# Attention, MoE and MoE on one core: half of block 0's loads into other tiles, and banks of their own for the last output sums

## The chip, the cores and the metric

The kernel runs on one core of a Trainium2 chip. A core has five engines that work side by side, each through its own instructions in order: TensorE (PE; its weight loads are listed as PEld), VectorE (DVE), ScalarE (ACT), GpSimd (POOL) and SyncE (SP, which here only issues DMAs). The metric is the device time of one execution in microseconds, the median over the runs shown; lower is better.

## What is computed

The reference chains three layers and returns float32; the MoE weights are float64:

```python
def reference(q, k, v, n_global, n_local, moe, moe2):
    x = attention(q, k, v)               # (2, 8, 768, 64): global keys < 8, local window of 96
    x = x.transpose(0, 2, 1, 3).reshape(1536, 512)
    h = x @ moe.w_in                     # 512 -> 2048
    P = a[0] + a[1] * h + a[2] * h**2 + a[3] * h**3
    Q = 1 + abs(b[0]) * abs(h) + abs(b[1]) * h**2
    x = (P / (Q + 1e-6)) @ moe.w_out     # 2048 -> 512
    h = x @ moe2.w_in                    # 512 -> 1024
    s = h * softmax(h)
    ln = (s - mean(s)) / sqrt(var(s) + 1e-6) * g_ln
    return ln @ moe2.w_out               # 1024 -> 512
```

Scores are masked to the first 8 keys and to the 96 keys up to the query's own, and get a bias that falls with the distance, with a slope of its own for each head.

## The kernel before

The 1536 tokens are cut into 12 tiles of 128. The **attention** of one tile is four units, each a pair of heads, numbered from 0 in the order in which they come: units 0 to 11 are block 0 (tiles 0 to 2), 12 to 23 block 1, and so on, four blocks of 384 tokens. A unit is loaded by two DMAs (`u_load`, lines 438 to 444): `qk`, its queries and keys, and `v`, its values. `u_front` multiplies them on PE (`L459`), takes the scores with bias and their extreme on DVE (`L464`), the exponential on ACT (`L471`), the reciprocal of the sum on DVE (`L476`, `L477`), and scales by it (`L482`) on DVE for the units in `NDVE` (3 to 11 among them) and on POOL for the others. `u_back` transposes (`L502`), copies (`L514`, ACT), multiplies by the values (`L509`), and copies the result into `x` as a high part (`L516`, ACT) and a remainder (`L99`, DVE).

**MoE 1** goes block by block over 16 slices of the hidden width. The high and low parts of the inputs and of the weights are multiplied apart (`L634`, `L636`, `L640`), the quotient P/Q is made on ACT, DVE and POOL (lines 660 to 679), and its product with the second weights (`L725`, `L726`, `L731`) sums in three PSUM banks. Block 0 does half of its slices first, is written to memory, and does the other half last. Weights come as 64-bit words, 512 KB for each DMA (`L541`), into four tiles `wst`, and are turned into float32 by ACT and DVE (`L565` to `L586`) and split into high (`L604`, ACT) and low (`L99`, mostly POOL).

**MoE 2** goes over the 12 tiles, in the order 3 to 11 and then 0 to 2; below they are counted from 0 in that order. For each: transposes of the input (`L791`), the hidden sums in two halves of 12 matmuls (`L810` to `L812`, `p2_h`), softmax and normalisation on DVE and ACT (`L832` to `L854`), eight transposes in two pieces of four (`L872`, `p2_tr`) with copies (`L880`) and remainders (`L99`), and the output sum of 24 matmuls in bank `y2` (`L894` to `L896`, `p2_o`), which ACT copies out (`L903`) for a DMA (`L905`). The last tile's sum is made in two halves of 256 columns.

**What sets the order.** `record` writes down every step as an operation with its engine, a length, the values that it reads and writes, and for new values the pool that they take a buffer from. `Plan.run` then goes through a list of ready operations and takes those whose turn comes first, by due times worked out backwards from the end; that writes each engine's order. Buffers are handed out from pools: `qk` has 3, `v` 4, `t` 9, `y` 4, `wst` 4; PSUM banks are pools too: `h` and `s` two each, `p`, `y0`, `y1`, `y2` one each. Values of one `line` get their buffers in the order in which they were written down. Where the plan leaves PE idle in its first 30 us, `fill` (`L337`) puts in small matmuls on the identity into a free bank; one of them in the source is two instructions of the trace. A load of a later weight is held until the hidden sum of the step before has run (`after`, line 541).

Four of the `t` tiles, t0 to t3, hold the tables from which the attention's bias is made (lines 383 to 417); apart from that `t` serves MoE 1's quotient, and `y` its finished sums.

## Time and profile before

| | us |
|---|---|
| median of 3 runs | 559.95 |
| lowest and highest | 559.59, 560.86 |
| the profiled execution | 558.11 |
| its span, first to last instruction | 556.3 |
| PE busy | 531.8 (96%), 2910 instructions |
| DVE busy | 446.0 (80%) |
| ACT busy | 393.0 (71%) |
| POOL busy | 182.5 (33%) |
| DMA, mean over the span | 101 GB/s |

A busy time is the time in which an engine has an instruction under way. The granted clock of PE is full for the whole of the work. The span has attention of block 0 up to about 44 us, MoE 1 with the attention of the other blocks beside it up to about 290, MoE 1 alone with the weights of MoE 2 up to about 400, and MoE 2 to the end. Times in the rows below are microseconds from the start of the span.

### The profile page before, as it was taken

How to read it: one execution, taken by the hardware profiler on the slowest of the kernel's cores; microseconds unless marked ns; L12 is line 12 of the kernel's file. 1: busy time of each engine (PE TensorE's matmuls, PEld its weight loads, DVE VectorE, ACT ScalarE, POOL GpSimd, SP SyncE). 2: the span in 40 equal slices, each digit the busy share in tenths (PEclk: the TensorE clock that was granted, in tenths of full speed). 3: DMA queues.
4: the chain of work that ended last, by engine and by line, in shares of the span. 5: the costliest groups of instructions: out<-in, count | busy, mean ns of one | idle time of the engine just before them, and what ended most of it. 6: DMA issues, size and time to landing. Idle time of an engine off the chain costs nothing.

```text
span 556.3 us, 8937 instructions
## 1 busy us (share of the span) xinstructions
PE 531.8 (96%) x2910; PEld 437.0 (79%) x2910; DVE 446.0 (80%) x1104; ACT 393.0 (71%) x911; POOL 182.5 (33%) x212
## 2 busy tenths in 40 slices
PE   7999999999999899999999999999999999999995
PEld 6668776877788678778788887888878788888874
DVE  4997999999999999878788999999876755455530
ACT  5688999898888878787778988898544543334330
POOL 2311665546456632122342644674510000000000
PEclk9999999999999999999999999999999999999999
DMA  7469662544354432211013322252101111000011
GB/s 252 130 201 341 195 219 86 185 135 153 104 182 154 151 96 98 73 48 48 1 38 114 133 77 75 77 180 87 57 20 38 39 38 58 20 19 20 19 39 43
DMA packets 28278, 56.24 MB, mean 101 GB/s; under 512 B 3520, under 2 KB 11968, under 8 KB 28224
## 3 DMA queue, kind: packets, MB, share of 16 engines
q1 hardware_dynamic: 28080, 55.59, 30.9%
q8 instruction: 25, 0.41, 0.3%
q14 instruction: 29, 0.24, 0.1%
q10 hardware_dynamic: 144, 0.00, 0.0%
HBM read 47.72 MB, written 7.86 MB: 100 GB/s over the span
## 4 chain that ended last, share of the span: by engine, by line
PE 55%; DVE 29%; ACT 10%; issue 4%; DMA 1%; POOL 0%; SPq 0%; ACTq 0%; DVEq 0%; POOLq 0%
PE pb L894 4%; PE pb L896 4%; PE pb L895 4%; PE pb L634 4%; PE pb L810 4%; PE pb L812 4%; PE pb L811 4%; PE pb L640 4%; PE pb L731 3%; PE pb L636 3%; PE pb L725 3%; DVE t L667 3%; PE pb L459 3%; DVE wst L574 3%; PE pb L726 3%
## 5 line engine op out<-in xcount | busy, mean ns | idle before, releaser
L99 POOL TENSOR_TENSOR g<-t,g 128x384 fp32r<-128x384 f32 x64 | 69.2, 1082 | 103.9 <-ACT g L677 91.7
L634 PE MATMUL pb<-x,w 128*128 128x384 f32 x256 | 89.3, 349 | 1.8 <-DVE t L667 1.8
L636 PE MATMUL pb<-x,w 128*128 128x384 f32 x256 | 86.1, 336 | 0.0
L725 PE MATMUL pb<-w,g 128*128 128x512 f32 x192 | 77.5, 404 | 4.2 <-ACT g L677 4.2
L726 PE MATMUL pb<-w,g 128*128 128x512 f32 x192 | 75.6, 394 | 0.5 <-POOL w L99 0.5
L99 POOL TENSOR_TENSOR w<-wst,w 128x512 fp32r<-128x512 f32 x42 | 57.2, 1364 | 42.7 <-ACT w L604 38.8
L640 PE MATMUL pb<-x,w 128*128 128x384 f32 x256 | 58.0, 347 | 0.1
L731 PE MATMUL pb<-w,g 128*128 128x512 f32 x192 | 57.7, 409 | 0.2 <-POOL g L99 0.2
L634 PEld LDWEIGHTS pb<-x,w 128*128 128x128 f32 x256 | 48.1, 188 | 8.6 <-DVE t L667 4.4
L471 ACT ACTIVATE e<-e,st 128x256 f32<-128x256 f32 (+1 forms) x96 | 46.3, 486 | 6.4 <-DVE st L464 6.4
L640 PEld LDWEIGHTS pb<-x,w 128*128 128x128 f32 x256 | 44.5, 188 | 7.1 <-issue 3.1
L636 PEld LDWEIGHTS pb<-x,w 128*128 128x128 f32 x256 | 48.1, 188 | 1.5
L725 PEld LDWEIGHTS pb<-w,g 128*128 128x128 f32 x192 | 36.0, 187 | 14.4 <-ACT g L677 7.3
L660 ACT ACTIVATE t<-pb,coef 128x384 f32<-128x384 f32 x64 | 42.7, 668 | 6.1 <-PE pb L640 6.1
L482 POOL TENSOR_SCALAR e<-e,st 128x256 f32<-128x256 f32 (+1 forms) x58 | 28.0, 495 | 54.4 <-DVE st L477 48.4
L669 ACT ACTIVATE t<-t,coef 128x384 f32<-128x384 f32 x64 | 39.6, 618 | 6.8 <-DVE t L667 6.6
L662 DVE TENSOR_TENSOR t<-t,pb 128x384 f32<-128x384 f32 x64 | 35.2, 549 | 11.1 <-ACT t L663 6.5
L677 ACT CAST g<-t 128x384 fp32r<-128x384 f32 x64 | 32.8, 512 | 16.0 <-DVE t L675 15.3
L880 ACT CAST lh<-pb 128x512 fp32r<-128x512 f32 x24 | 13.9, 592 | 42.5 <-PE pb L872 42.5
L459 PE MATMUL pb<-qk 64*128 64x256 f32 (+3 forms) x192 | 41.3, 393 | 2.7 <-DVE st L464 1.0
L667 DVE SCALAR_TENSOR_TENSOR t<-pb,coef,t 128x384 f32<-128x384 f32 x64 | 39.2, 613 | 5.2 <-ACT pb L666 4.8
L671 DVE SCALAR_TENSOR_TENSOR t<-t,t 128x384 f32<-128x384 f32 x64 | 40.6, 634 | 1.3 <-ACT t L670 1.3
(113 smaller groups left out, 1293.2 us busy)
## 6 DMA issues: line engine op xcount, KB each, us to landing
wst<-in_w_in SPq DMA_DIRECT2D x24, 512.0 KB, 4.0
wst<-in_w_out SPq DMA_DIRECT2D x24, 512.0 KB, 3.7
qk<-in_qkv SPq DMA_DIRECT2D x40, 256.0 KB, 2.7
v<-in_qkv SPq DMA_DIRECT2D x40, 128.0 KB, 2.5
y_d<-y SPq DMA_DIRECT2D x12, 256.0 KB, 2.5
y<-y_d SPq DMA_DIRECT2D x12, 256.0 KB, 2.6
out<-wst SPq DMA_DIRECT2D x11, 256.0 KB, 2.0
qk<-in_qkv SPq DMA_DIRECT2D x8, 192.0 KB, 3.7
```

The source lines that it names most:

```text
L99: eng.tensor_tensor(out=out, in0=a, in1=hi.bitcast(F32), op=ALU.subtract)
L459: pe.matmul(out=score(h), lhsT=a[r, h * 128:(h + 1) * 128], rhs=a[r, 256:256 + w], start=True, stop=True)
L471: act.activation(out=e[:, h, 0:w], in_=e[:, h, 0:w], func=AF.Exp, scale=-1.0, bias=st[:, h:h + 1], accum_out=st[:, 2 + 2 * h:3 + 2 * h])
L634: pe.matmul(out=pb[:, g.h.slot, 0:n], lhsT=wt[wh.slot][:, cs[p]], rhs=xt[x[p][0].slot][:, 0:n], start=(p == 0), stop=False)
L636: pe.matmul(out=pb[:, g.h.slot, 0:n], lhsT=wt[wl.slot][:, cs[p]], rhs=xt[x[p][0].slot][:, 0:n], start=False, stop=False)
L640: pe.matmul(out=pb[:, g.h.slot, 0:n], lhsT=wt[wh.slot][:, cs[p]], rhs=xt[x[p][1].slot][:, 0:n], start=False, stop=(p == 3))
L660: op("ACT", 0.2 + 0.46 * k, lambda: act.activation(out=T(g.c), in_=h(), func=AF.Identity, scale=coef[:, 3:4], bias=coef[:, 2:3]), r=[g.h], ...
L667: op("DVE", 0.2 + 0.41 * k, lambda: stt_(out=T(g.a), in0=h(), scalar=coef[:, 5:6], in1=T(g.b), op0=ALU.mult, op1=ALU.add), r=[g.h, g.b], n ...
L671: op("DVE", 0.15 + 0.41 * k, lambda: stt_(out=T(g.a), in0=T(g.a), scalar=1.0 + 1e-6, in1=T(g.b), op0=ALU.add, op1=ALU.mult), r=[g.b], w=[g ...
L725: pe.matmul(out=pb[:, y[i].slot, :], lhsT=gt[g.gh.slot][:, c], rhs=wt[wh.slot], start=g.first, stop=False)
L726: pe.matmul(out=pb[:, y[i].slot, :], lhsT=gt[g.gh.slot][:, c], rhs=wt[wl.slot], start=False, stop=False)
L731: pe.matmul(out=pb[:, y[i].slot, :], lhsT=gt[g.gl.slot][:, c], rhs=wt[wh.slot], start=False, stop=g.last)
```

## The change

In block 0 every second unit (odd numbers) loads its `qk` into a tile of pool `y` and its `v` into one of pool `t`. The values have lines of their own there (`qk0`, `v0`). In `p2_h` the first half of a tile's hidden sum takes both of its banks and the second half writes on, and the sums wait until all weights but the last two have been scaled (`scaled[:-2]`). In `p2_o` the tile before the last sums in bank `y1`, and the second half of the last one in a bank of pool `s`. The branch `ROOT`, another way to make Q, is off, so its code is left out here, and an unused tile `cf` of four columns is added.

```diff
+ROOT, EARLY, ENDS = False, (0,), True
...
+    def aside(u):
+        return u.j in EARLY and u.k % 2 == 1
+
+    def qk_of(u):
+        return yt[u.qk.slot] if aside(u) else qkt[u.qk.slot]
+
+    def v_of(u):
+        return tt[u.v.slot] if aside(u) else vt[u.v.slot]
+
     def u_load(u):
-        u.qk, u.v = Val("qk"), Val("v")
+        u.qk, u.v = (Val("y", "qk0"), Val("t", "v0")) if aside(u) else (Val("qk"), Val("v"))
...
-    nconv, nlo = [0], [0]
+    nconv, nlo, scaled = [0], [0], []
...
-        op("ACT", 0.63, scale, r=[st], new=[bank] + list(new), lead=WLEAD, tag="wsc")
+        scaled.append(op("ACT", 0.63, scale, r=[st], new=[bank] + list(new), lead=WLEAD, tag="wsc"))
...
-               new=[o.h[half]] if half else [o.h[0]], occ=2.76, tag="h2")
+               **{"w" if half else "new": o.h[1:] if half else o.h}, occ=2.76, after=scaled[:-2], tag="h2")
...
-        b, ot = Val("y2"), Val("wst", "ot")
+        ot = Val("wst", "ot")
+        bs = [Val("y2")] if n == 1 else [Val("y2"), Val("s" if ENDS else "y2")]
+        if ENDS and o.k == NTILE - 2:
+            bs = [Val("y1")]
+        if n == 2 and not ENDS:
+            bs[1] = bs[0]
```

Since the plan is made anew, the order of all engines moves. Three places follow. On SyncE, after the two small loads at the start of the program, the order before was (`qk0` to `qk2` and `v0` to `v3` are the buffers of a unit's two loads, `wst` a weight):

```order
L441 DMA qk0_204<-in_qkv 128x384
L441 DMA qk1_205<-in_qkv 128x384
L441 DMA qk2_206<-in_qkv 128x384
L443 DMA v0_207<-in_qkv 128x128
L443 DMA v1_208<-in_qkv 128x128
L443 DMA v2_209<-in_qkv 128x128
L443 DMA v3_210<-in_qkv 128x128
L541 DMA wst0_156<-in_w_in 128x1024
L541 DMA wst1_157<-in_w_in 128x1024
L541 DMA wst2_158<-in_w_in 128x1024
L441 DMA qk0_204<-in_qkv 128x384
```

The same place on SyncE now (lines 473 and 475 are 441 and 443):

```order
L473 DMA qk0_204<-in_qkv 128x384
L473 DMA y0_189<-in_qkv 128x384
L473 DMA qk1_205<-in_qkv 128x384
L473 DMA y1_190<-in_qkv 128x384
L473 DMA qk2_206<-in_qkv 128x512
L475 DMA v0_207<-in_qkv 128x128
L473 DMA y2_191<-in_qkv 128x512
L475 DMA t4_164<-in_qkv 128x128
L475 DMA v1_208<-in_qkv 128x128
L475 DMA t5_165<-in_qkv 128x128
L473 DMA y3_192<-in_qkv 128x512
L473 DMA qk0_204<-in_qkv 128x512
```

Unit 3's `qk` has moved from behind three weights to the fourth place, and the first weight comes ten rows later than before.

On VectorE, behind the reciprocal of unit 2, the order before was (`x` a unit's result, `e3` and `st3` the scores and sums of unit 3; 569 to 574 are a weight's conversion):

```order
L99 TENSOR_TENSOR x1_174<-pb_89,x0_173 128x128
L569 SCALAR_TENSOR_TENSOR pb_89<-pb_89,wst0_156 128x512
L570 SCALAR_TENSOR_TENSOR pb_89<-wst0_156,pb_89 128x512
L99 TENSOR_TENSOR x3_176<-pb_89,x2_175 128x128
L574 SCALAR_TENSOR_TENSOR wst0_156<-wst0_156,pb_89 128x512
L99 TENSOR_TENSOR x5_178<-pb_89,x4_177 128x128
L569 SCALAR_TENSOR_TENSOR pb_89<-pb_89,wst1_157 128x512
L570 SCALAR_TENSOR_TENSOR pb_89<-wst1_157,pb_89 128x512
L464 ISA e3_214,st3_219<-pb_89,bt6_202 128x128
```

The same place on VectorE now:

```order
L496 ISA e3_214,st3_219<-pb_89,bt6_202 128x128
L496 ISA st3_219 128x1
L496 ISA e3_214,st3_219<-pb_89,bt7_203 128x128
L496 ISA st3_219 128x1
L103 TENSOR_TENSOR x1_174<-pb_89,x0_173 128x128
L496 ISA e0_211,st4_220<-pb_89,bt0_196 128x256
L496 ISA st4_220 128x1
L496 ISA e0_211,st4_220<-pb_89,bt1_197 128x256
L496 ISA st4_220 128x1
L508 TENSOR_SCALAR st3_219<-st3_219 128x2
```

The conversions of two weights have left this place, and units 3 and 4 have come forward.

On TensorE, between the output sums of tiles 8 and 9 of MoE 2, the order before was (`lh0`, `lh1` and `ll0`, `ll1` are the two tiles' transposed inputs, `wst0` the normalised rows of tile 10):

```order
L894 MATMUL pb_89<-w31_123,lh0_2943 128x512
L895 MATMUL pb_89<-w30_122,lh0_2943 128x512
L896 MATMUL pb_89<-w31_123,ll0_2945 128x512
L872 MATMUL pb_89<-ident_65,wst0_156 128x128 x4
L894 MATMUL pb_89<-w17_109,lh1_2944 128x512
L895 MATMUL pb_89<-w19_111,lh1_2944 128x512
```

The same place on TensorE now:

```order
L942 MATMUL pb_89<-w30_122,lh0_2925 128x512
L943 MATMUL pb_89<-w31_123,ll0_2927 128x512
L941 MATMUL pb_89<-w17_109,lh1_2926 128x512
L942 MATMUL pb_89<-w19_111,lh1_2926 128x512
L943 MATMUL pb_89<-w17_109,ll1_2928 128x512
```

The four transposes between the two sums have moved ahead of both.

## Rows read from the trace of the kernel before

**Rows 1.** By stage: stretch, length; PE, PEld, DVE, ACT, POOL busy; clock; DMA share; GB/s.

```profile
7.86:20.00 12.14, 11.00 (x84) 8.38 (x82) 8.85 (x35) 10.33 (x35) 4.75 (x9) 1.00 0.72 257
20.00:43.66 23.66, 22.76 (x176) 16.04 (x176) 22.09 (x97) 18.08 (x64) 5.05 (x7) 1.00 0.60 185
43.66:60.00 16.34, 15.69 (x106) 13.03 (x104) 12.93 (x39) 14.17 (x39) 4.28 (x6) 1.00 0.84 289
60.00:200.00 140.00, 133.21 (x748) 107.43 (x747) 136.19 (x332) 124.95 (x299) 80.85 (x96) 1.00 0.49 154
200.00:290.00 90.00, 90.00 (x525) 72.28 (x524) 75.48 (x201) 72.37 (x174) 25.39 (x29) 1.00 0.19 58
430.00:544.00 114.00, 112.79 (x554) 93.71 (x552) 61.19 (x147) 46.16 (x94) 0.00 (x0) 1.00 0.09 31
```

**Rows 2.** Timeline of PE in block 0: start, duration, line, operation, count.

```profile
16.00 0.49 PE L459 MATMUL pb<-qk 64*128 64x128 f32 x4
16.42 2.27 PE L337 MATMUL pb<-ident 128*128 128x128 f32 x18
...
43.66 0.42 PE L634 MATMUL pb<-x,w 128*128 128x384 f32 x1
```

**Rows 3.** DMA issues of SyncE; last row: landing times of `L441` up to 20 us.

```profile
4.97 1.38 SPq L541 DMA_DIRECT2D wst<-in_w_in  x3
6.61 0.33 SPq L441 DMA_DIRECT2D qk<-in_qkv  x1
...
DMA to landing us min/median/max: 2.7/3.8/6.0
```

**Rows 4.** Waits of DVE, 7.5 to 44 us: total us, times, longest.

```profile
DVE x L99 <- ACT x L516: 1.2, 3, 0.7
DVE e L464 <- ACT bt L417: 1.2, 3, 0.5
DVE st L476 <- ACT e L471: 1.1, 3, 0.4
DVE pb L569 <- ACT pb L565: 0.8, 1, 0.8
```

**Rows 5.** Timeline of DVE in block 0, rows of normalisations and of one reduction.

```profile
19.17 1.55 DVE L482 TENSOR_SCALAR e<-e,st 128x128 f32<-128x128 f32 x2
...
37.38 1.64 DVE L482 TENSOR_SCALAR e<-e,st 128x256 f32<-128x256 f32 x2
...
42.98 0.41 DVE L464 CUSTOM_DVE_ANT_0 e<-pb,bt 128x256 f32<-128x256 f32 x1
...
43.77 0.17 DVE L476 TENSOR_SCALAR st<-st 128x2 f32<-128x2 f32 x1
...
44.24 0.61 DVE L482 TENSOR_SCALAR e<-e,st 128x256 f32<-128x256 f32 x2
```

**Rows 6.** Timeline of POOL at the same times.

```profile
19.38 1.27 POOL L99 TENSOR_TENSOR w<-wst,w 128x512 fp32r<-128x512 f32 x1 [0.51 <-ACT w L604]
...
37.60 1.27 POOL L99 TENSOR_TENSOR w<-wst,w 128x512 fp32r<-128x512 f32 x1 [12.80 <-ACT w L604]
```

**Rows 7.** Timeline of PE in MoE 2, with idle time before and its releaser.

```profile
408.69 1.09 PE L872 MATMUL pb<-ident,wst 128*128 128x128 f32 x8 [0.77 <-DVE wst L854]
...
432.45 0.66 PE L872 MATMUL pb<-ident,wst 128*128 128x128 f32 x4 [0.80 <-DVE ll L99]
...
531.60 0.50 PE L894 MATMUL pb<-w,lh 128*128 128x512 f32 x1 [0.24 <-ACT wst L903]
...
543.44 0.39 PE L896 MATMUL pb<-w,ll 128*128 128x512 f32 x1
544.50 0.39 PE L894 MATMUL pb<-w,lh 128*128 128x256 f32 x1 [0.68 <-ACT wst L903]
```

**Rows 8.** Timelines of ACT and SyncE in MoE 2.

```profile
424.42 1.12 ACT L859 ACTIVATE pb<-wst,st 128x1024 f32<-128x1024 f32 x1 [2.40 <-DVE st L839]
...
550.91 0.81 SPq L905 DMA_DIRECT2D out<-wst  x2
```

More of the change, by code (lines that the diff above doesn't have):

```diff
@@ L417, in bias_pair, with root_log, root_end @@
             act.mul(bt[h], dz, -8.0 * SLOPE[h])
+    vcf = Val()
+    cf = const.tile([128, 4], F32, name="cf")
+    def root_log():
+        act.activation(out=cf[:, 1:2], in_=cf[:, 0:1], func=AF.Ln)
+        act.activation(out=cf[:, 1:2], in_=cf[:, 1:2], func=AF.Exp, scale=0.5)
+    def root_end():
+        dve.reciprocal(out=cf[:, 2:3], in_=cf[:, 1:2])
+        dve.scalar_tensor_tensor(out=cf[:, 1:2], in0=cf[:, 0:1], scalar=cf[:, 2:3], in1=cf[:, 1:2], op0=ALU.mult, op1=ALU.add)
+        dve.tensor_scalar(out=cf[:, 1:2], in0=cf[:, 1:2], scalar1=0.5, scalar2=None, op0=ALU.mult)
+        dve.reciprocal(out=cf[:, 2:3], in_=cf[:, 1:2])
+        dve.tensor_tensor(out=cf[:, 3:4], in0=cf[:, 2:3], in1=coef[:, 4:5], op=ALU.mult)
     op("POOL", 0.9, bias_iota, new=vt0)
@@ L508, in pv @@
                     v0 = k * 128 + h * 64
-                    pe.matmul(out=pb[h * 64:(h + 1) * 64, u.xp.slot, 0:128], lhsT=vt[u.v.slot][:, v0:v0 + 64],
+                    pe.matmul(out=pb[h * 64:(h + 1) * 64, u.xp.slot, 0:128], lhsT=v_of(u)[:, v0:v0 + 64],
                               rhs=ptt[:, c:c + 128], start=(k == 0), stop=(k == n - 1))
@@ L659, in e_ops @@
         stt_ = dve.scalar_tensor_tensor
-        op("ACT", 0.2 + 0.46 * k, lambda: act.activation(out=T(g.c), in_=h(), func=AF.Identity, scale=coef[:, 3:4], bias=coef[:, 2:3]),
-           r=[g.h], new=[g.c], tag="c")
-        op("DVE", 0.14 + 0.41 * k, lambda: dve.tensor_tensor(out=T(g.c), in0=T(g.c), in1=h(), op=ALU.mult), r=[g.h], w=[g.c], tag="ch")
-        op("ACT", 0.15 + 0.42 * k, lambda: act.activation(out=T(g.b), in_=h(), func=AF.Abs, scale=coef[:, 4:5]), r=[g.h], new=[g.b], tag="abs")
@@ L899, in p2_o @@
         cs = [slice(i * w, (i + 1) * w) for i in range(n)]
-        parts = [op("PE", 5.52 / n + 0.3, lambda c=c: mm(c), r=[o.lh, o.ll] + [v for f in range(8) for v in W["o2", f]],
-                    **{"w" if i else "new": [b]}, occ=5.52 / n, tag="o") for i, c in enumerate(cs)]
         for i, c in enumerate(cs):
-            op("ACT", 0.59 / n, lambda c=c: act.copy(wst[ot.slot].bitcast(F32)[:, c], pb[:, b.slot, c]), r=[b],
+            b = bs[i]
+            op("PE", 5.52 / n + 0.3, lambda c=c, b=b: mm(c, b), r=[o.lh, o.ll] + [v for f in range(8) for v in W["o2", f]],
+               **{"w" if i and b is bs[0] else "new": [b]}, occ=5.52 / n, tag="o")
+        for i, c in enumerate(cs):
+            b = bs[i]
+            op("ACT", 0.59 / n, lambda c=c, b=b: act.copy(wst[ot.slot].bitcast(F32)[:, c], pb[:, b.slot, c]), r=[b],
                **{"w" if i else "new": [ot]}, tag="ot")
```

36 lines of the change are left out of this document (27 added, 9 removed).

## Prediction

> **What bounds the kernel now.** I read the busy time by stages first [rows 1], then the first 44 us on TensorE, SyncE and VectorE, then the waits of TensorE in MoE 2. In [rows 1] the binding engine changes from stage to stage. From 60 to 200 us VectorE is busy for 136.19 of 140 us; from 200 to 290 us TensorE for 90.00 of 90, and from 430 to 544 us for 112.79 of 114. Neither kind of stretch can take in a delay: what reaches 60 us earlier or later reaches the end earlier or later, unless the order of work behind it changes. Slack that a reordering can win lies ahead of that: VectorE is busy for 8.85 of the 12.14 us up to 20 us, and for 12.93 of 16.34 between 43.66 and 60 us.
>
> The first stretch is the attention of block 0, twelve units. TensorE starts the first hidden matmul of MoE 1 at 43.66 us, when the last of them is done [rows 2]. TensorE is not what sets that: it runs fillers, for instance 18 instructions in 2.27 us ahead of the scores of unit 4 [rows 2], 0.126 us each. The loads have a part in it. The score tiles have three buffers, so the load of unit 3 is issued at 6.61 us, after the first score matmul, and behind three weight loads of 512 KB; loads of this line take 2.7 to 6.0 us to land in the first 20 us [rows 3], so it may land as late as 12.6. Its matmul runs at 16.00 us [rows 2]. VectorE fills part of this hole with weight conversions. So the hole is not all lost time, and its price is what VectorE really waited: from 7.5 to 44 us 1.2 us for the copy x of a unit (`L516`), 1.2 for the bias tables, 1.1 for exponentials and 0.8 for a weight's scaling [rows 4], 4.3 in all.
>
> **The change part by part.** *Loads of block 0.* The counts of compute instructions and DMAs stay as they are; only 19 pairs of fillers fall away (32 for 51). Units 1, 3, 5, 7, 9 and 11 load into y and t tiles, so only half of the units still take turns in the three score and four value buffers, and seven units are on their way before the first weight. On SyncE the first weight load now stands behind 17 loads of units in place of 7. Three issues there take 1.38 us [rows 3], so the ten more make it 10 x 0.46 = 4.6 us later. Its conversion has moved on VectorE too, behind the scores of unit 7, and is hidden by them. If it landed later still, VectorE would wait in its order, and units 8 to 11, which come next on it, with it.
>
> On VectorE the score reductions now follow each other. Of the 3.1 us that were not spent on the bias tables (those stay: ScalarE's order is unchanged up to there) I take 1.8 as won. The bounds are 0 (each wait turns up at another reciprocal, since the chain of reduction, exponential and reciprocal is as long as before) and 3.1; I take the middle, somewhat up, since the later waits on `L516` fall when more units are in flight.
>
> Two units of block 1 leave this stretch too. Before, the reductions of units 12 to 15 stand ahead of the last rounding remainder of block 0, now those of 12 and 13 alone. The reductions of one unit take from 42.98 to 43.77 us, 0.79, and its reciprocal two instructions of 0.17 [rows 5]: two units and one reciprocal are 1.9 us, which move behind the start of MoE 1. There VectorE has 16.34 - 12.93 = 3.4 us of idle time [rows 1], which hides them; without that cover they would cost 1.9 again. So the first hidden matmul comes 1.8 + 1.9 = 3.7 us earlier, at about 40.0 us. The fillers say much the same from the other side: 19 pairs at 2 x 0.126 = 4.8 us less of hole to fill.
>
> One cost in this stretch goes by luck. The normalisation of a unit on VectorE takes 0.61 us for two instructions, but 1.55 and 1.64 where GpSimd subtracted a weight's halves at the same time (from 19.38 and from 37.60, 1.27 each); in both cases they end together [rows 5, 6]. That is about 1.0 us twice. Four such subtractions stand in this stretch, before and now. I leave it at two meetings; none would give 2 us more, four take 2 us.
> [...]
>
> *Order in MoE 2.* The first half of the hidden sums now claims both banks, and the order there changes much, on TensorE, which has no slack: each wait is paid in full. Before, 24 hidden matmuls, transposes, and 24 output matmuls alternate. Now halves of 12 are parted by transposes, and three times two output sums follow each other on bank y2, which ScalarE must empty between. The second and third (tiles 1 and 2, tiles 5 and 6) have a transpose between them, as tiles 8 and 9 had before, where the wait was 0.24 us [rows 7]; tiles 8 and 9 now have nothing between, as the last two sums had, 0.68 us [rows 7]. That is 2 x 0.24 + 0.44 = 0.9 us. Transposes of a tile that come three pieces in a row waited 0.80 us once for a bank [rows 7]; now there are two such places, 0.8 us more. The wait of 0.77 us for the first normalised tile [rows 7] goes, since those transposes now stand a half later. Together +0.95 us; bounds -0.8 and +3.5, since a copy can also stand behind a square of 1.12 us on ScalarE [rows 8].
>
> *Banks of the last sums.* Tile 10 sums in y1 and the second half of tile 11 in a bank of its own. The first matmul of tile 11 started at 544.50, 1.06 us after the last of tile 10 in place of the usual 0.23 [rows 7]: 0.83 us go. The copy of its first half is then done while the second is summed, and the last output DMA, now the second of a pair that SyncE issues in 0.81 us [rows 8], goes half of that, 0.4 us, sooner. That is -1.23 us, with little doubt.
>
> **The sum.** -3.7 + 0.95 - 1.23 = -4.0 us on the profiled execution of 558.11 us (span 556.3 and 1.8 around it): 554.1. The median of the runs, 559.95, lies 1.84 us above that execution, so the forecast is 556.0.
>
> **The rivals.** *The early gain is hidden anyway.* The weights wait instead of the units: conversions that VectorE did in the hole, where it was busy for 8.85 us [rows 1], must be done later, in a stretch where it is busy for 22.09 of 23.66 us, and the chain of reduction, exponential and reciprocal, not the load, turns out to have set the pace; of the waits nothing is won, and the two moved reductions push the first activations of MoE 1 back by as much. Then about 0.6 us of the 3.7 is left: 559.95 - 0.6 + 0.95 - 1.23 = 559.1. For it: only 3.1 us of wait are there at all. Against it: 19 pairs of fillers fewer, and the 3.4 us of idle time after 43.66 us.
>
> *MoE 2 gives it back, and more.* This is the slower case. Three places with output sums in a row and three with transposes in a row each wait not 0.24 to 0.80 us but for a copy, a remainder and a 1.12 us square in ScalarE's queue, some 1.1 us more each: 6 x 1.1 = 6.6, so 562.6. It turns slower than before by 0.2% when those six cost 5.1 us more than counted, 0.85 each. For it: TensorE has 1.2 us of idle time in 114 there, so the order before was better than one can expect of a new one. Against it: ScalarE is busy for 46.16 of 114 us, so the queue is mostly short [rows 1].
>
> [...] All four subtractions meet a normalisation: 558.0, still faster; none: 554.0.
>
> *The change does not do what it says:* a load of block 0 into a t tile could wait for the bias tables, which live in t0 to t3 at first. The order excludes it but for unit 11, whose turn comes long after.
>
> **How the numbers follow.** Forecast with its spread of port meetings 0.70, all of it faster; hidden gain 0.16, of which 0.13 within 0.2% and 0.03 faster; MoE 2 gives back 0.14, of which 0.02 ends within 0.2% and 0.12 slower. A measurement of this kernel tells about 0.2% (1.1 us) from no change. So faster 0.73, same 0.15, slower 0.12. The range: all bounds in the good direction (no port meeting, 3.1 us of waits won, MoE 2 at -0.8) give 556.0 - 2.0 - 1.3 - 1.75 = 551.0, all in the bad one over 561. I cut both by what seldom comes together: 552.3 to 560.4.
>
> **What would show it.** Right: the score matmul of unit 3 near 10 to 11 us, the first hidden matmul near 40 us, VectorE above 9.5 of 12.14 us in the first stretch, 60 us reached with the same MoE 1 work done as before at 63 to 64, and no wait of the last sum near its start. Wrong: a first hidden matmul at 43 us (the loads did not matter), VectorE idle for longer than 3.4 us right after it (the moved work was not hidden), normalisations of 1.5 us in more than two places, or TensorE below 111 of 114 us in MoE 2. Waits of TensorE on the copy `L903` beyond 1.2 us in total would show the order there as the price.

## The result, and the profile after

The change made the kernel slower: 566.09 us median of 4 runs (564.62 to 566.16), where the kernel before has 559.85 (559.59 to 560.86), a ratio of 1.0108 (1.0086 to 1.0129). The forecast was 556.0 with a range of 552.3 to 560.4, so direction and range were both wrong. The profiled execution took 566.08 us; its span is 563.9 us, 7.6 more than before. (The medians are 6.2 us apart. The profiled execution of before, 558.11 us, lies 1.7 under its median, that of after on its median.) TensorE is busy for 531.9 us (531.8 before), although it has 38 filler instructions less to run (2872 instructions for 2910): slower work at the start (2.1 us) and near 188 us (an estimated 1.7 us, below) fills most of their place, and the 7.6 us are idle time.

The lines of before have other numbers now: `L99` is `L103`, `L459` `L491`, `L464` `L496`, `L514` `L546`, `L516` `L548`, `L574` `L606`, `L634` `L666`, `L662` `L704`, `L667` `L709`, `L725` `L767`, `L872` `L914`, `L894` `L941`, `L903` `L953`; kernels with edits further up have 3 to 7 more. The stages, with the columns of [rows 1]:

```profile
7.86:20.00 12.14, 11.90 (x80) 8.84 (x80) 6.79 (x41) 9.59 (x39) 2.16 (x6) 1.00 0.97 317
41.67:60.00 18.33, 16.15 (x108) 13.84 (x107) 15.08 (x49) 15.83 (x42) 7.82 (x12) 1.00 0.79 261
60.00:200.00 140.00, 129.60 (x728) 105.19 (x727) 133.21 (x321) 121.22 (x292) 79.39 (x92) 0.99 0.47 146
200.00:290.00 90.00, 89.94 (x522) 71.80 (x521) 76.23 (x202) 71.80 (x173) 25.29 (x28) 1.00 0.20 62
430.00:544.00 114.00, 111.39 (x541) 91.71 (x540) 62.62 (x154) 46.15 (x95) 0.00 (x0) 1.00 0.09 31
```

Against [rows 1], VectorE (the third busy time) has lost 2 us at the very start (6.79 for 8.85) and 3 us between 60 and 200 us, where it is the engine that sets the pace (133.21 for 136.19). TensorE has lost 1.4 us in MoE 2 (111.39 for 112.79).

**The start.** The timeline of TensorE, then a row of VectorE and the first hidden matmul:

```profile
5.65 0.80 PE L491 MATMUL pb<-qk 64*128 64x128 f32 x4 [1.05 <-DMA qk<-in_qkv]
6.38 4.63 PE L341 MATMUL pb<-ident 128*128 128x128 f32 x20
10.94 0.58 PE L491 MATMUL pb<-y 64*128 64x128 f32 x4
...
41.67 0.52 PE L666 MATMUL pb<-x,w 128*128 128x384 f32 x1
```

```profile
11.66 0.29 DVE L496 CUSTOM_DVE_ANT_0 e<-pb,bt 128x128 f32<-128x128 f32 x1 [3.00 <-PE pb L491]
```

The 20 fillers between the scores of units 0 and 1 took 4.63 us, 231 ns each. In the profile of before the same 20 took 2.50 us, from 5.84 on. Unit 1's scores stand behind them in TensorE's order, so VectorE waited 3.00 us for these scores. Even so the first hidden matmul came 2.0 us earlier than in [rows 2].

**MoE 1.** What VectorE waited for from 100 to 200 us, after (total us, times, longest):

```profile
DVE t L709 <- ACT pb L708: 1.5, 3, 0.7
DVE x L103 <- ACT x L548: 1.0, 3, 0.6
DVE t L704 <- ACT t L702: 0.5, 2, 0.3
DVE t L704 <- ACT t L705: 0.4, 1, 0.4
DVE st L508 <- ACT e L503: 0.2, 1, 0.2
```

and the same of before:

```profile
DVE t L667 <- ACT pb L666: 0.8, 3, 0.4
```

That is 3.6 us in place of 0.8. Near 188 us the granted clock of TensorE also fell, to 0.58 over 4 us. Its timeline, and the windows around it (columns as in [rows 1]):

```profile
186.56 0.66 PE L541 MATMUL pb<-pt,v 128*64 128x128 f32 x8 [0.73 <-ACT pt L546]
188.59 0.77 PE L767 MATMUL pb<-w,g 128*128 128x512 f32 x1 [1.37 <-ACT g L719]
189.16 0.63 PE L768 MATMUL pb<-w,g 128*128 128x512 f32 x1
189.59 0.63 PE L767 MATMUL pb<-w,g 128*128 128x512 f32 x1
```

```profile
184.00:188.00 4.00, 2.10 (x16) 1.33 (x16) 3.96 (x8) 3.02 (x7) 1.28 (x1) 1.00 0.68 231
188.00:192.00 4.00, 3.41 (x10) 2.75 (x11) 3.93 (x9) 2.80 (x7) 3.16 (x4) 0.58 0.41 125
```

From 188.6 to 192.0 us the granted clock is 0.51, and the matmuls of `L767` and `L768` start 0.43 us apart and not 0.23 as at 198 us. Ahead of that lies a stretch in which TensorE worked for 2.10 of 4 us, at 1.00. Estimated from the clock, 3.4 us x (1 - 0.51), the same work would take 1.7 us less at 1.00. Of the four runs of the change, the three near 566.1 us have a mean granted clock of 0.993 or 0.994, and the one of 564.62 us has 1.000.

**The end of MoE 1, and MoE 2.** Rows of TensorE's timeline, with its longest waits there and the start of the last two output sums:

```profile
376.83 0.44 PE L666 MATMUL pb<-x,w 128*128 128x384 f32 x1 [1.58 <-DVE t L709]
...
418.93 0.47 PE L852 MATMUL pb<-w,yh 128*128 128x512 f32 x1 [1.12 <-DVE wst L606]
...
439.55 0.66 PE L914 MATMUL pb<-ident,wst 128*128 128x128 f32 x4 [0.79 <-DVE ll L103]
...
459.33 0.50 PE L941 MATMUL pb<-w,lh 128*128 128x512 f32 x1 [0.85 <-ACT wst L953]
...
509.14 0.50 PE L941 MATMUL pb<-w,lh 128*128 128x512 f32 x1 [0.24 <-ACT wst L953]
...
540.72 0.50 PE L941 MATMUL pb<-w,lh 128*128 128x512 f32 x1 [0.73 <-ACT wst L953]
...
552.49 0.39 PE L943 MATMUL pb<-w,ll 128*128 128x512 f32 x1
552.72 0.28 PE L941 MATMUL pb<-w,lh 128*128 128x256 f32 x1
```

The last output sum starts 0.23 us behind the sum before it, where [rows 7] had 1.06: that part of the change does what it should.

Where the same step has the same matmuls in both kernels, its start can be followed through the span. After minus before: first hidden matmul -2.0 us; 40th of MoE 1's 64 hidden steps (280 us) +4.7; last hidden step of MoE 1 +5.4; output sum of tile 10 +9.1; last sum +8.2; last matmul +8.1; end +7.6. So the front gained 2.0, MoE 1 up to 200 us lost 6.7, what lies between 300 us and tile 10 lost 4.4, and the banks at the end won back 1.5.

**Where the front's gain went.** It was gone by the 4th hidden step, which starts at 55.67 us before and at 57.49 after. VectorE from the first hidden step to the 4th, and from the start of the span to the 26th (198.11 us before, 202.80 after), each time before and then after:

```profile
43.66:55.67 12.01, 8.83 (x28) 1.00 0.99 343
0.00:198.11 198.11, 181.81 (x519) 1.00 0.55 176
```

```profile
41.67:57.49 15.82, 12.64 (x41) 1.00 0.83 279
0.00:202.80 202.80, 181.88 (x519) 0.99 0.54 171
```

Between the first and the 4th step VectorE works 3.8 us longer than before and is idle for the same 3.18 us: what had moved behind the first hidden matmul was not taken up by idle time there. Up to the 26th step it has run the same 519 instructions with the same busy time, so the 4.69 us by which this step comes late are its idle time, 20.92 us for 16.30. Of the 4.62 us more, 1.69 lie ahead of the first hidden matmul (the slow fillers), none between there and the 4th step, and 2.92 between the 4th and the 26th. (Steps in between are no fair measure: the 20th comes 0.66 us ahead of before again, but with 4.6 us less of VectorE's work done by then.)

### The profile page after: what moved, and what is told of

Read it like the earlier page. It is cut to its first block, busy times and chain, and to the rows that moved or that the text cites. A ratio compares the mean times of both kernels' runs of the same rounds, so it can differ in the third digit from the quotient of the medians.

```text
span 563.9 us, 8864 instructions
## 1 busy us (share of the span) xinstructions
PE 531.9 (94%) x2872; PEld 435.4 (77%) x2872; DVE 448.8 (80%) x1104; ACT 392.8 (70%) x911; POOL 183.2 (32%) x212
## 3 DMA queue, kind: packets, MB, share of 16 engines
HBM read 47.72 MB, written 7.86 MB: 99 GB/s over the span
## 4 chain that ended last, share of the span: by engine, by line
PE 49%; DVE 31%; ACT 13%; issue 5%; DMA 1%; POOL 0%; SPq 0%; ACTq 0%; DVEq 0%
PE pb L767 4%; PE pb L666 3%; PE pb L672 3%; PE pb L768 3%; PE pb L852 3%; PE pb L854 3%; PE pb L853 3%; DVE wst L606 3%; PE pb L773 3%; PE pb L668 3%; PE pb L941 3%; PE pb L943 3%; PE pb L942 3%; PE pb L491 3%; DVE t L709 3%
## 5 line engine op out<-in xcount | busy, mean ns | idle before, releaser
L103 POOL TENSOR_TENSOR g<-t,g 128x384 fp32r<-128x384 f32 x64 | 69.1, 1079 | 114.4 <-ACT g L719 101.3
L666 PE MATMUL pb<-x,w 128*128 128x384 f32 x256 | 89.6, 350 | 3.0 <-DVE t L709 2.8
L767 PE MATMUL pb<-w,g 128*128 128x512 f32 x192 | 79.1, 412 | 6.3 <-ACT g L719 6.1
L768 PE MATMUL pb<-w,g 128*128 128x512 f32 x192 | 76.2, 397 | 0.0
L103 POOL TENSOR_TENSOR w<-wst,w 128x512 fp32r<-128x512 f32 x42 | 57.3, 1363 | 46.1 <-ACT w L636 46.0
L773 PE MATMUL pb<-w,g 128*128 128x512 f32 x192 | 57.7, 408 | 0.1
L666 PEld LDWEIGHTS pb<-x,w 128*128 128x128 f32 x256 | 48.1, 188 | 11.2 <-DVE t L709 7.3
L767 PEld LDWEIGHTS pb<-w,g 128*128 128x128 f32 x192 | 36.3, 189 | 18.4 <-ACT g L719 11.1
L514 POOL TENSOR_SCALAR e<-e,st 128x256 f32<-128x256 f32 (+1 forms) x58 | 28.9, 511 | 52.8 <-DVE st L509 34.9
L704 DVE TENSOR_TENSOR t<-t,pb 128x384 f32<-128x384 f32 x64 | 35.1, 549 | 11.7 <-ACT t L705 6.4
L709 DVE SCALAR_TENSOR_TENSOR t<-pb,coef,t 128x384 f32<-128x384 f32 x64 | 39.3, 614 | 5.2 <-ACT pb L708 3.9
L717 DVE SCALAR_TENSOR_TENSOR t<-t,coef,t 128x384 f32<-128x384 f32 x64 | 42.5, 663 | 1.1
L941 PE MATMUL pb<-w,lh 128*128 128x512 f32 (+1 forms) x104 | 40.0, 385 | 1.8 <-ACT wst L953 1.8
L768 PEld LDWEIGHTS pb<-w,g 128*128 128x128 f32 x192 | 36.5, 190 | 5.9
## 6 DMA issues: line engine op xcount, KB each, us to landing
x_d<-x SPq DMA_DIRECT2D x8, 192.0 KB, 2.7
```

The costliest lines, as they stand in the source:

```text
L103: eng.tensor_tensor(out=out, in0=a, in1=hi.bitcast(F32), op=ALU.subtract)
L666: pe.matmul(out=pb[:, g.h.slot, 0:n], lhsT=wt[wh.slot][:, cs[p]], rhs=xt[x[p][0].slot][:, 0:n], start=(p == 0), stop=False)
L709: op("DVE", 0.2 + 0.41 * k, lambda: stt_(out=T(g.a), in0=h(), scalar=coef[:, 5:6], in1=T(g.b), op0=ALU.mult, op1=ALU.add), r=[g.h, g.b], n ...
L717: op("DVE", 0.2 + 0.43 * k, lambda: stt_(out=T(g.c), in0=T(g.c), scalar=coef[:, 0:1], in1=T(g.b), op0=ALU.add, op1=ALU.mult), r=[g.b], w=[ ...
L767: pe.matmul(out=pb[:, y[i].slot, :], lhsT=gt[g.gh.slot][:, c], rhs=wt[wh.slot], start=g.first, stop=False)
L768: pe.matmul(out=pb[:, y[i].slot, :], lhsT=gt[g.gh.slot][:, c], rhs=wt[wl.slot], start=False, stop=False)
```

## Experiments: the parts of the change one by one

Up to about the 1060th row of TensorE's order (late in MoE 1) the early loads alone set the order; the rule on scaled weights (`scaled[:-2]`) acts from there on, the claim of both banks from about the 1390th row, in MoE 2, and the banks of the last sums leave nearly every row where it was. So the parts can be run one by one. Theory A: the early loads are the price. Theory B: the order in MoE 2. Theory C: the rule on the scaled weights.

**Early loads alone.** The edit, against the changed kernel:

```diff
-ROOT, EARLY, ENDS = False, (0,), True
+ROOT, EARLY, ENDS = False, (0,), False
-               **{"w" if half else "new": o.h[1:] if half else o.h}, occ=2.76, after=scaled[:-2], tag="h2")
+               new=[o.h[half]] if half else [o.h[0]], occ=2.76, tag="h2")
```

> Only the early loads of block 0 (the hidden sums and the last output sums of MoE 2 as before). The order of all engines is that of the changed kernel up to about the 1060th row of TensorE, late in MoE 1, and that of the kernel before at the end. Theory A, the early loads are the price: their order wins 2.0 us up to the first hidden matmul and TensorE idles 1.7 us more up to 60 us, 2.5 more up to 104, 0.9 more up to 204, and 1.7 us go to a stretch of half clock near 189 us; so about 5 us slower than before, 565 (563.5 to 566.5). Theory B, the order in MoE 2 is the price: 556 to 558.

Measured: 562.75 us (562.48 to 563.25), 1.0076 (1.0061 to 1.0092), under the 563.5 to 566.5 us of theory A and far above those of theory B. Against the profile of before, the first hidden matmul comes 2.1 us earlier (41.55), the 40th hidden step 4.5 us later, and everything behind it 4.4 to 4.5 us later to the end. So the early loads are somewhat over half of the loss in the trace (4.4 of 7.6 us), as theory A has it; the start is the same as after (4.62 us for the 20 fillers), and so is the stretch of lower clock (0.58).

**The claim of both banks alone** (`EARLY` empty, `ENDS` off, no `after`):

```diff
-               **{"w" if half else "new": o.h[1:] if half else o.h}, occ=2.76, after=scaled[:-2], tag="h2")
+               **{"w" if half else "new": o.h[1:] if half else o.h}, occ=2.76, tag="h2")
```

> Only the claim of both banks by the first half of a hidden sum of MoE 2. The order differs from before from about row 1390 of TensorE on, in MoE 2. In the changed kernel TensorE idled 1.2 us more between 405 and 480 us. Theory A: 561 (560 to 562). Theory B: 565 to 567, with waits of the output sums on the copy out of their bank of over 5 us in total.

Measured: 560.80 us (559.41 to 564.12), 1.0042 (1.0023 to 1.0060). From the end of MoE 1 to the last sum it loses 2.2 us. (At the end of MoE 1 it is 0.75 us ahead of before, although the order up to there is the same; the last section shows where that comes from.) Two rows of its timeline carry most of the loss:

```profile
408.55 0.66 PE L914 MATMUL pb<-ident,wst 128*128 128x128 f32 x4 [1.65 <-DVE wst L896]
...
464.46 0.50 PE L941 MATMUL pb<-w,lh 128*128 128x512 f32 x1 [0.86 <-ACT wst L953]
```

The wait for the first normalised tile has grown from 0.77 us [rows 7] to 1.65, and the second of two output sums in a row waits 0.86 us for the copy of the first. Theory B has a part of the loss, not the 6 us it expected.

**The banks of the last sums alone** (`EARLY` empty, `p2_h` as before).

> Only the banks of the last output sums (tile 10 in y1, second half of tile 11 in a bank of its own). All theories: the wait of 0.68 us at the last sum goes, and the last DMA leaves 0.4 us sooner: 1.2 us faster, 558.7 (558 to 559.5). If the copy of the first half does not hide: 559.3.

Measured: 557.28 us (555.79 to 559.34), 0.9973 (0.9957 to 0.9990), 1.5 us faster. The trace shows why one profile can deceive here:

```profile
5.45 0.80 PE L491 MATMUL pb<-qk 64*128 64x128 f32 x4 [0.85 <-DMA qk<-in_qkv]
6.18 4.34 PE L341 MATMUL pb<-ident 128*128 128x128 f32 x20
```

In this execution the order at the start is that of before, yet the fillers took 4.34 us. The first hidden matmul came at 45.33 us, 1.67 later than in [rows 2], and every step up to tile 10's output sum kept 1.5 to 1.7 us of it.

**The rule on scaled weights alone** (`EARLY` empty, `ENDS` off, the old claims with `after=scaled[:-2]`).

> Only the rule that the hidden sums of MoE 2 wait until all weights but two are scaled. The order differs from before from about row 1060 of TensorE on. In the changed kernel TensorE idled 2.5 us less between 290 and 375 us and 3.1 more between 375 and 405. Theory A: near no change, 560.5 (559 to 562). Theory C, this rule is the price, since it moves weight conversions on VectorE into the last slices of MoE 1: 563 to 566.

Measured: 568.92 us (567.73 to 570.61). With the old claims and this order the plan can hand a half of a hidden sum one bank while its matmuls write another, so some sums are spoilt and the order of MoE 2 is that of neither kernel (TensorE waits 5.29 us at one place that neither has). The time says nothing of the rule itself; the next run gives its price.

**All but the early loads** (`EARLY` empty, the rest as changed).

> The whole change but the early loads. If the parts add up: 1.0108 less 0.0076 for the early loads, 1.0032, 560.7 where before is 558.9; both banks (2.3 us) and the banks of the last sums (1.7 us less) leave 0.6, so the rule on the scaled weights then costs 1.2 us. Rival, the rule on the scaled weights costs 4 us or more where it is not covered by the early loads: 563 or more.

Measured: 561.92 us (559.95 to 562.24), 1.0053 (1.0033 to 1.0073). Both banks (0.0042) and the last banks (-0.0027) make 0.0015 of that, so the rule on scaled weights costs about 0.004, some 2.1 us, with an uncertainty as large as these intervals. The trace agrees: between the 49th hidden step and tile 10's sum it loses 4.4 us, the claim of both banks alone 2.2. Its waits there are those of after, 1.59 us for a quotient on VectorE near 373 us and 1.12 for a weight's conversion near 415. That the rule pulls conversions on VectorE ahead of the last quotients of MoE 1 would explain them, but is not shown. Theory C has a part too, more than the 1.2 us that adding up had given and less than the rival's 4. The early loads, 1.0076, and all the rest, 1.0053, make 1.0129 together, against 1.0108 (1.0086 to 1.0129) for the whole: within the uncertainty of the three intervals.

## Experiments: why the early loads lose

**More fillers at the start, with the early loads alone.** If the fillers run slow because TensorE idled before, two pairs more ahead of unit 0 should mend it:

```diff
     def fill(n, spare):
-        for _ in range(n if spare else 0):
+        grown.append(0)
+        for _ in range((n + 2 if len(grown) == 1 else n) if spare else 0):
```

> The early loads alone, with 8 in place of 6 pairs of fillers ahead of unit 0's score matmul, so that TensorE idles less there (1.03 us before). All else is ordered as in the run of the early loads alone (562.75). Theory D, the pace at the start is a price of its own: the 20 fillers behind unit 0 take 2.5 us and not 4.62, the 3.0 us wait of VectorE for unit 1's scores goes, the first hidden matmul comes near 39.6 us instead of 41.55, and the end 2 us sooner, 560.7. Theory E, VectorE waits later for the same: first hidden matmul earlier, end unchanged, 562.0 to 563.0. If the fillers keep their half pace: no change anywhere.

Measured: 561.70 us (560.14 to 562.59), 1.0057 (1.0037 to 1.0077). The profiled execution, 560.24 us, has the start at full pace:

```profile
5.69 0.49 PE L494 MATMUL pb<-qk 64*128 64x128 f32 x4 [0.24 <-DMA qk<-in_qkv]
6.11 2.50 PE L344 MATMUL pb<-ident 128*128 128x128 f32 x20
8.54 0.74 PE L494 MATMUL pb<-y 64*128 64x128 f32 x4
...
39.43 0.53 PE L669 MATMUL pb<-x,w 128*128 128x384 f32 x1
```

The first hidden matmul is 2.12 us earlier than without these fillers, and the last matmul 2.18: what the start gives, the end keeps, one to one. In the trace theory D stands and E falls. The median gained only 1.05 us, not the 2 that D gave, and the six runs spread over 2.4 us, so probably not all of them had the full pace. But with a first hidden matmul 4.2 us earlier than before, the profiled execution still ends 2.1 us later than before's. So the slow start is a part of the loss, not its cause.

**The same fillers with the banks of the last sums, no early loads.**

> Only the banks of the last output sums, with the same two extra pairs of fillers at the start. Theory D: the start is at full pace in every run, so the runs lie closer together than those of the banks alone (555.79 to 559.34) and near their lower end, 556.3 median. Rival: the start is slow in few of its runs, or the extra fillers hold unit 0 back by 0.2 to 0.5 us: 557.3 to 557.8.

Measured: 556.15 us (555.54 to 556.95), 0.9956 (0.9939 to 0.9974). The six runs lie within 1.4 us of each other where the twelve of the banks alone spread over 3.6, as theory D says, though in the profiled one the fillers still took 3.27 us.

**The clock near 188 us.** Five pairs of fillers ahead of the output step that begins there:

```diff
+                if e == "PE" and fill and o.tag == "y" and o.fn.__name__ == "hi":
+                    self.his = getattr(self, "his", 0) + 1
+                    if self.his == 20:
+                        spare = [b for p in ("p", "y2", "y1", "y0", "s", "h") for f, b in self.pools[p] if f <= idle and b not in [v.slot for v in o.vals if v.pool in BANKS]]
+                        fill(5, spare)
                 o.fn()
```

> The early loads alone, with 5 pairs of fillers on TensorE ahead of the output step that starts at 188.52 us after 1.34 us of idle time, and whose six matmuls run at 0.43 us each and not 0.23, with the granted clock at 0.58 in that stretch. Theory F, the fall of the clock costs the end: the six run at 0.23 us, the granted clock stays at 1.00, the end comes 1.7 us sooner, 561.0. Theory G, VectorE sets the pace there and hides it: clock full, time within 0.5 us of 562.75.

Measured: 561.05 us (559.55 to 561.84), 1.0041 (1.0025 to 1.0058). The same place:

```profile
186.76 1.38 PE L346 MATMUL pb<-ident 128*128 128x128 f32 x10 [0.22 <-DVE wst L611]
187.89 0.48 PE L772 MATMUL pb<-w,g 128*128 128x512 f32 x1
188.21 0.40 PE L773 MATMUL pb<-w,g 128*128 128x512 f32 x1
...
190.22 0.44 PE L671 MATMUL pb<-x,w 128*128 128x384 f32 x1 [0.26 <-DVE t L714]
```

The clock stays at 1.00 in these windows and the matmuls start 0.23 us apart. Against the early loads alone the steps are 0.64 us earlier ahead of this place (the start went better in this execution) and 1.30 behind it, so the clock gave back 0.66 us of the 1.7; the rest turned into waits for VectorE. The median is the 561.0 us of theory F, but by the trace the start has a part in that, so the answer lies between F and G.

**None, some and all of the early loads, with one start.** From here on 10 pairs of fillers stand ahead of unit 0's scores and 6 behind them, and the banks of the last sums are on; `p2_h` is as before. Only `aside` differs: never, units 1 and 3, all odd units, and all odd units for queries and keys only.

```diff
-        return u.j in EARLY and u.k % 2 == 1
+        return u.j in EARLY and u.k in (1, 3)
```

None:

> No early loads, the banks of the last output sums, and 10 pairs of fillers ahead of unit 0's scores and 6 behind them (6 and 10 before). VectorE takes unit 0's scores at 7.86 us only, so TensorE may come to them up to about 7 us. Theory D: the second group of fillers runs at full pace in every run, the first hidden matmul comes at 43.7 us, the runs lie within 1.2 us of each other, 555.7 median. Rival: unit 0's scores, held back by about 0.6 us, hold VectorE back too: 556.3 or more.

All:

> The same start and banks with the early loads of all six odd units. Theory D and the trace of the early loads with more fillers (first hidden matmul 4.2 us earlier than before, end of MoE 1 2.3 us later): first hidden matmul near 39.4 us, 2.2 us slower than with the same start and no early loads, 557.9. If the early loads only lost by the slow start: 553 to 555.

Units 1 and 3:

> The same start and banks with units 1 and 3 alone loaded early, so that 4 loads fewer stand ahead of the first weight on SyncE than with all six. Theory H, the loads ahead of the weights and the work that they move are the price: a third of the 2.2 us, 556.4. Theory L, the new order of MoE 1 up to 195 us is a draw that has little to do with the number of loads: anywhere from 554 to 559, with the waits of VectorE for ScalarE between 100 and 195 us telling where.

Queries and keys only:

> The same start and banks with only the queries and keys of the odd units loaded early, their values as before. Theory H: between none and all, 556.4 to 557.3, with a first hidden matmul between 39.4 and 43.7 us. Theory L: anywhere from 554 to 559, and not in the order of the first hidden matmul.

| early loads | first hidden matmul | 40th hidden step | VectorE busy, 60 to 200 us | median us | ratio to before |
|---|---|---|---|---|---|
| (before) none | 43.66 | 280.13 | 136.19 | | 1 |
| none | 43.74 | 280.19 | 136.25 | 556.22 | 0.9939 (0.9914 to 0.9964) |
| units 1 and 3 | 40.47 | 282.08 | 133.53 | 559.31 | 1.0008 (0.9986 to 1.0031) |
| all odd units | 39.21 | 282.08 | 133.48 | 560.09 | 1.0000 (0.9984 to 1.0016) |
| queries, keys only | 39.63 | 285.77 | 133.48 | 565.87 | 1.0111 (1.0083 to 1.0139) |

With 10 pairs the first group runs on until unit 0's scores are there, and the fillers behind it run at full pace in three of these four profiles (1.60 us for 12; 1.91 with units 1 and 3). The runs without early loads still spread over 2.4 us (555.64 to 558.08), where theory D gave 1.2. Theory H falls: two units loaded early lose as much by 280 us as six, and loading queries alone loses most. All three ways win 3.2 to 4.5 us up to the first hidden matmul, and all three are behind by 280 us. What they share stands in the fourth column. The medians of none and all are 3.9 us apart, more than the traces at the 40th step (1.9); what the other executions lost beyond that is not shown. The rows of VectorE, 100 to 150 us, none and then all (columns: busy, clock, DMA share, GB/s):

```profile
100.00:150.00 50.00, 48.76 (x121) 1.00 0.48 152
```

```profile
100.00:150.00 50.00, 46.45 (x108) 1.00 0.43 140
```

**Other orders behind the same front.** Is that idle time the price of the loads, or of the order that the planner draws behind them? The last four kernels change the planner's weights, one `lead` for each kind of operation (some 50 numbers), two sets with all early loads and two without any. Unlike in the table above the claim of both banks is on, in all four; the start and the last banks are as there.

```diff
+    for o in plan.ops:
+        o.lead += FIT.get(o.tag, 0.0)
     plan.settle(ROUNDS)
```

With early loads:

> All six odd units loaded early, the same start, both banks claimed at once, the banks of the last sums, and other weights for the planner (the lead of each kind of operation), chosen for this set of operations, so that the order behind the front is another. Theory L, the front gain was lost to the order of MoE 1, not to the loads: first hidden matmul near 39.3 us as with the early loads before, and the end below the 556.2 of the run without early loads, 552 to 555. Theory M, VectorE has the same work to do whatever comes first, so the front gain cannot reach the end: 556 or more, and no better than the run without early loads and with weights of its own.

> The same with a second, unlike set of weights. Theory L: first hidden matmul within 0.3 us of the other set, the end over 1 us away from it, anywhere from 552 to 558. Theory M: 556 or more.

Without:

> No early loads, the same start, both banks claimed at once, the banks of the last sums, and weights chosen for this set of operations. A control: without it a gain of the other two could be one of the weights alone. Theory L: 553 to 557, first hidden matmul near 43.7 us. Theory M: as fast as the best with early loads or faster.

> The control with a second set of weights: 553 to 557 by theory L, with the two controls over 1 us apart; by theory M as fast as the best with early loads or faster.

| early loads, set | first hidden matmul | 40th hidden step | VectorE busy, 60 to 200 us | median us | ratio to before |
|---|---|---|---|---|---|
| all, first | 40.15 | 277.88 | 136.44 | 555.83 | 0.9945 (0.9925 to 0.9965) |
| all, second | 39.84 | 278.38 | 134.76 | 559.12 | 0.9998 (0.9986 to 1.0010) |
| none, first | 41.79 | 279.69 | 135.40 | 556.95 | 0.9962 (0.9950 to 0.9975) |
| none, second | 40.68 | 277.93 | 136.74 | 554.75 | 0.9922 (0.9902 to 0.9942) |

With the first set the early loads are 2.2 us ahead of before at the 40th hidden step, where with the old weights they were 1.95 behind: 4.2 us between two orders with the same loads. VectorE's row from 100 to 200 us, all early loads, with the old weights and with the first set:

```profile
100.00:200.00 100.00, 94.45 (x216) 0.98 0.46 145
```

```profile
100.00:200.00 100.00, 97.30 (x227) 1.00 0.46 150
```

So where MoE 1 stands at 280 us is a matter of the order, as theory L says. Yet the lead is not the front's gain come through. VectorE's rows from the first hidden step to the 4th and from the start to the 26th, with the first set:

```profile
40.15:52.19 12.04, 11.01 (x34) 1.00 0.95 354
0.00:194.97 194.97, 181.18 (x519) 1.00 0.55 178
```

Ahead of the first hidden matmul VectorE is idle for as long as before (9.23 us for 9.16). The lead comes from the stretch behind it: 1.03 us of idle time up to the 4th step, where before and after have 3.18, and 13.79 in place of 16.30 up to the 26th. Here the moved work did go into idle time. The reason that theory M gives, the same work whatever comes first, holds as well: 519 instructions in 181.18 us for 181.81. In their times neither theory did well. 555.83 us lies above the 552 to 555 of theory L and just under the 556 of M, and the second set's 559.12 above the 558 of L. The controls lie in L's 553 to 557, but with their first hidden matmul at 41.79 and 40.68 and not near 43.7, and the best of them is faster than the best with early loads, as M says: without early loads the second set has the best time of all, 554.75. The early loads bring nothing that an order of their own does not bring without them. Two sets each are too few to say that they never would.

## Why the prediction was wrong, point by point

**The front, -3.7 us.** The size at the first hidden matmul was near, its make-up was not. With a start at full pace it comes 4.2 to 4.5 us earlier. VectorE's rows from 7.86 us to the first hidden matmul, before and then with all early loads and the mended start, tell what it consists of:

```profile
7.86:43.66 35.80, 30.94 (x131) 1.00 0.64 209
```

```profile
7.86:39.21 31.35, 27.45 (x125) 1.00 0.76 254
```

Of 4.45 us, 3.5 are work that is no longer there (30.94 became 27.45) and 0.96 are idle time (4.86 became 3.90). So the 1.8 us of waits won were set too high: half of them turned up elsewhere, which lies within the bounds that the text named. Two reductions moved, as counted; and no normalisation met a subtraction of GpSimd, neither after (11 rows of 0.48 to 0.62 us up to 50 us) nor here, where [rows 5, 6] had two at 1.55 and 1.64. That is the 2 us which the text had for the luckiest case. That the two meet at a port, as the forecast words it, is shown by no run. The runs show the durations: 1.0 us more for each of the two normalisations beside a subtraction in [rows 5, 6], none here, where nothing met, and 0.4 to 0.9 us more for one of two instructions near 139 us, in the last section. By the 26th hidden step VectorE's busy time is that of before within 0.3 us (182.04 us with all early loads and the mended start), so what the front saved by not meeting was paid elsewhere.

**"There VectorE has 16.34 - 12.93 = 3.4 us of idle time [rows 1], which hides them".** This is the step that failed first. The work that moved out of the front was not hidden: between the first and the 4th hidden step VectorE was idle for 3.18 us before and for 3.18 after, and worked 3.8 us longer. So the 1.9 us of the two moved units, half of the -3.7, came back in full, and with the 0.96 us of idle time alone the front would have given a quarter of its term. That it could have been hidden shows in the order with other weights for the planner, where the same loads left 1.03 us of this idle time; the order of the change did not use it.

**The start was taken as given.** The prediction did not ask whether the profile's own start was typical. It was not: with the order of before, the 20 fillers took 2.50 us in two profiles and 3.92, 4.34 and 4.63 us in three (these are before and four kernels of the parts), and 4.06 to 4.63 in all three with the early loads and the old fillers. The price at the first hidden matmul is 1.2 to 2.1 us, and where the order behind it stayed the same it reached the end. Against the profile of before, after pays +2.1 us on a term that was not in the sum. Against the median of before it pays less: the sum added 1.84 us for the distance of that profile from the median, which a slow start in the other runs would account for, though no trace shows it.

**"What reaches 60 us earlier or later reaches the end earlier or later, unless the order of work behind it changes".** This is the second step that failed. The order did change, up to about 200 us, and the text put that at nothing: it priced only the place at 43.66 to 60 us. VectorE's busy share there, 136.19 of 140 us, was read as a law of the stage. It was the merit of one order: the new one has 133.21, with 3.6 us of waits for ScalarE from 100 to 200 us in place of 0.8, and 2.92 us more of idle time between the 4th and the 26th hidden step. Both steps together turned -2.0 us into +4.7 (3.8 by the 4th step, 2.9 behind it). The first rival came nearest, with 559.1 us: that the moved reductions push the first activations of MoE 1 back by as much, and that about 0.6 us is left, is near what the rows show (0.96). That weights come too late is not: from 7 to 200 us no engine has a wait for a weight's DMA in the profile of after, and two units loaded early cost as much as six. And it had no loss behind that point. The slower rival, MoE 2 giving back 6.6 us by waits for copies, had a right place and a wrong price: all waits on the copy `L953` are 1.8 us.

**MoE 2, +0.95 us.** Measured: both banks 2.2 us and the rule on scaled weights 2.1 us. The wait for the first normalised tile was forecast to go (-0.77); with both banks alone it grew to 1.65, and in the whole change a wait of 1.12 us for a weight stands in its place. Two sums in a row with a transpose between were counted at 0.24 us each and took 0.24 and 0.85; those with nothing between were counted at 0.68 and took 0.73. Three pieces of transposes in a row waited 0.79 us once, not twice more. The 2.2 us of the banks lie inside the text's bounds (-0.8 to 3.5), the 4.3 us of both do not. The rule on scaled weights was quoted in the change and had no price at all; by the trace without early loads it acts from the 49th hidden step on, at the end of MoE 1.

**The last banks, -1.23 us.** Right: 0.9973, 1.5 us, with an interval of 0.6 to 2.4; the last sum starts without a wait, and from the last matmul to the end of the span it is 5.4 us in place of 5.9.

**The signs named.** Unit 3's scores came at 13.29 us and not at 10 to 11, VectorE worked for 6.79 of the first 12.14 us and not above 9.5, the waits on the copy `L953` are 1.8 us in total and not below 1.2, and the work that before has done at 55.67 us is done at 57.49, where the forecast had 60 us reached with the work of 63 to 64: four signs against the forecast. The first hidden matmul at 41.67 lay between right and wrong. TensorE's 111.39 of 114 us in MoE 2 and the normalisations were on the right side. So was VectorE's idle time right behind the first hidden matmul, 3.25 us up to 60 us, but that sign was set wrongly: had the moved work been hidden, the 3.4 us would have shrunk. No sign was named for the stretch from 60 to 200 us.

**The chances.** The slower case had 0.12, with one place (MoE 2) as its mechanism. Each of three replanned stretches lost some 2 us or more, and the forecast had treated only one as free to do so. Where a change makes the planner draw a tuned order anew, the order behind each place that it touches is a term of its own, with a range of some 4 us here.

## What to carry to other kernels

An engine that is busy for 97% of a stage is so by the merit of one order: when a change makes a planner draw that order again, price each redrawn stage as a loss, and tune the planner's weights for the new set before judging the change. Work that leaves one stretch is won only if idle time in a later one takes it: follow the busy time and the idle time of the engine that sets the pace up to a step that has the same work done in both kernels. Compare the first profile with others of the same start before taking a duration from it, and give the start its own term. Of a change with several parts, run each alone: here one part of a few lines was worth 1.5 us, and it was hidden under 8 us of loss from the others.

## What the runs showed of the hardware

The pace of TensorE's first instructions varies between executions of one order. After 12 fillers at 244 ns each and 0.80 to 0.86 us of idle time, the next 20 ran at 125 ns each in two executions and at 196 to 231 ns in three; with 10 pairs ahead and no idle time, 12 fillers behind ran at 133 ns each in six of eight. The record of the granted clock reads 1.00 in all of these windows, so here the durations tell and the clock column does not. Nor does the quicker pace come at the same moment. With 6 pairs ahead the 20 fillers ran at 125 ns each from 5.84 us on before, and at 217 ns from 6.18 to 10.52 us with the last banks alone, in the same order there. With 10 pairs ahead and the second set of weights, the 12 behind ran at 133 ns from 6.13 us on without early loads and at 153 ns from 6.97 us on with them. What brings the quicker pace is not shown.

After the change the granted clock fell near 188 us (0.58 over 188 to 192 us) behind three waits of TensorE, of 0.39, 0.73 and 1.37 us, in a stretch of 4 us in which it worked for 2.10. With fillers in the last of these waits (early loads alone) it stayed at 1.00, and that gave the end 0.66 us of the estimated 1.7.

Two executions with one order can keep their distance to within 0.1 us over hundreds of microseconds (with the last banks alone, 1.67 us behind before at the first hidden matmul and 1.68 at the first hidden sum of MoE 2). That is what made it possible to follow a gain or a loss from the place where it arose to the end.

But not always. Before, and with the claim of both banks alone, VectorE and GpSimd run the same order up to 200 us, and near 139 us a quotient on VectorE starts within 10 ns of a remainder on GpSimd. Before:

```profile
138.88 1.42 DVE L671 SCALAR_TENSOR_TENSOR t<-t,t 128x384 f32<-128x384 f32 x1
138.87 1.01 POOL L99 TENSOR_TENSOR g<-t,g 128x384 fp32r<-128x384 f32 x1
```

and with both banks:

```profile
138.97 0.55 DVE L713 SCALAR_TENSOR_TENSOR t<-t,t 128x384 f32<-128x384 f32 x1
138.96 1.43 POOL L103 TENSOR_TENSOR g<-t,g 128x384 fp32r<-128x384 f32 x1
```

One of the two takes 0.4 to 0.9 us longer, and which one differs between executions of one order. Where VectorE goes through unhindered, the hidden steps behind this place come 0.8 us sooner, so a difference of that size in one trace is not yet one of the kernel.
